# Six staging slots for the experts' weights instead of four, on one TensorE-bound core

## The chip, the core and the metric

The kernel runs on one core of one Trainium2 chip. A core has TensorE (PE; its weight loads are shown apart as PEld), VectorE (DVE), ScalarE (ACT), GpSimd (POOL) and SyncE (SP), whose queue issues most DMAs. Each engine takes its instructions in order from its own queue, and semaphores tie the queues together. The metric is the device time of one execution in microseconds; a version's time is the median of its runs.

## The reference, cut to what matters

The first step is a circular convolution along the sequence by FFT; the second is a mixture of 8 experts, of which each token uses two.

```python
X = np.fft.rfft(x, axis=1)                      # x: 8 x 2496 x 256
y = np.fft.irfft(X * F, n=x.shape[1], axis=1)   # F: the filter

logits = x @ w_gate                             # x: y as 19968 x 256
noisy_logits = logits + np.log1p(np.exp(x @ w_noise)) * noise
top2 = np.argpartition(-noisy_logits, 2, axis=1)[:, :2]
...                                             # top2_w: softmax of the two
for e in range(8):
    for k in range(2):
        mask = top2[:, k] == e
        h = np.maximum(x[mask] @ w1[e], 0.0)    # w1: 256 x 1024
        out[mask] += top2_w[mask, k, None] * (h @ w2[e])   # w2: 1024 x 256
```

## The kernel before

**Two streams.** The FFT is done batch by batch as dense transforms on PE (`s1`, `kg0` to `kg2`, `t3`, `i2`), which writes the filtered tokens to a DRAM tile `y`, computes the gates, and writes lists of token numbers per expert to a DRAM tile `lst` (`route`: a transpose on PE at L1015, a few DVE operations, and an accumulating write at L1027 on POOL's queue). As soon as lists of a batch are there, expert work on them starts (`expert`), and the FFT steps of later batches are woven into it. From some 1450 us on only expert work is left.

**Expert work.** It goes in blocks of up to 512 tokens of one expert. Per block, `read_list` loads the list (`lt`, L1048) and converts it to `ids` (L1056), `gather` fetches the tokens by an indirect DMA (L1094), `turn` transposes them (first blocks: a copy on POOL at L1146 and PE at L1154; later ones by DMA, L1125) and splits them into a high and a low part (`mxh` on ACT, L1157; `mxl` on DVE, L1158). For each eighth of the hidden layer PE makes 6 matmuls (L126 to L128) into a PSUM tile `hps`; ACT takes the ReLU `hh` (L1249) and DVE the remainder `hl` (L1250). Then PE multiplies by the second layer (`yps`; L126 to L128, and L1280 with L1281 in the later blocks), ACT scales by the gate (L1287), DVE adds in the later ones (L1289), and POOL's queue adds the rows to `out` in DRAM (L1290).

**The weights.** They come in quarters of 128 x 512 fp32 (256 KB). `front` loads four quarters of `w1` and four of `w2` for each new expert block, through `load_w`, whose DMAs stand in SP's queue (L1176; L1183 to L1191 for the smaller blocks at the end, of which `wb` at L1191 and `wc` have tiles of their own). Each quarter lands in a staging slot, ACT casts it to the high part (L1204) and DVE subtracts to get the low part (L1206). This last reading frees the slot. The cast also needs a free one of the four buffers of `w1h`/`w1l` or `w2`, which PE's matmuls on the quarter before free.

**The staging area.** `setup` makes one tile `stage`; `slot(nm)` deals out pieces of it in turn. There are four kinds: `wst` (weights, 4 slots of 512 columns), `xg` (gathered tokens, 4), `yo` (results, 4) and `x32` (transposed tokens, 2). Early on, the first 5120 columns also hold an intermediate of the FFT (`F`).

**The order.** It is partly written out by hand (`pin`, `after`), and for the rest a scheduler puts every engine's instructions in order when the kernel is built, by the waits and costs that it models. So another number of slots can move instructions on all engines. Both versions are built with `dynamic_dma_scratch_size=4096`, the ring of descriptors.

Of the kernel before, what the change touches and what calls it, by code (L numbers as in the profile page):

```python
# [10 lines left out]
F32 = mybir.dt.float32  # L11
# [43 lines left out]
YW = D + E  # L55
# [93 lines left out]
class Moe:  # L149
# [40 lines left out]
    def setup(self):  # L190
        tc, nc, io, cp = self.tc, self.nc, self.io, self.cp
        self.z = cp.tile([128, YW], F32, name="z")
        nc.gpsimd.memset(self.z, 0.0)
        self.ident = cp.tile([128, 128], F32, name="ident")
        make_identity(nc, self.ident)
        self.cV = cp.tile([128, 128], F32, name="cf")
        hl = cp.tile([128, 732], R32, name="hl")
        self.small = cp.tile([128, 64], F32, name="small")
        self.half = cp.tile([128, 4 * LR + 2 * NG + 256], F16, name="half")
        self.sum16 = cp.tile([128, 128], F16, name="sum16")  # L200
        self.new16 = cp.tile([128, 1], F16, name="new16")
        self.val16 = cp.tile([128, 2, SW], F16, name="val16")
        for t in (self.sum16, self.new16, self.val16):
            nc.gpsimd.memset(t, 0.0)
        self.fr = cp.tile([128, 2, 20, 128], F32, name="fr")
        self.fi = cp.tile([128, 2, 20, 128], F32, name="fi")
        self.wg = cp.tile([128, 2, 32], F32, name="wg")
        self.sgn = cp.tile([64, 20], F32, name="sgn")


        self.stage = cp.tile([128, 4096 + 4 * YW], F32, name="stage")
        self.turns = {}
        self.F = [self.stage[:, 2560 * h:2560 * h + 2560].rearrange("p (k b) -> p k b", k=CB) for h in range(2)]
        cm = self.P.tile([128, 494], F32, name="cm", tag="tl", bufs=3)
        self.cm = cm
        self.rC, self.rM, self.rD = cm[:RP, 0:120], cm[:, 120:248], cm[:120, 248:365]
        self.cW = cm[:, 366:494]
        self.hl = hl
        nc.vector.memset(self.wg, 0.0)
        self.cC = (hl[:RP, 0:120], hl[:RP, 120:240])  # L220
        self.cM = (hl[:, 240:368], hl[:, 368:496])
        self.cD = (hl[:120, 496:613], hl[:120, 614:731])
        sm = self.small
        self.tri, self.ones, self.key = self.half[:, -256:-128], self.half[:, -128:], sm[:, 0:8]
        self.lastok, self.iota = sm[:, 8:9], sm[:, 32:32 + SW]
        self.epart, self.ebase, self.eoff = sm[:, 9:10], sm[:, 10:11], sm[:, 16:24]
        self.base = cp.tile([128, E], F32, name="base")
        self.cnt = cp.tile([E, 1], F32, name="cnt")
        self.done = cp.tile([E, 1], F32, name="done")
        self.nblk = cp.tile([E, 1], F32, name="nblk")  # L230
        for t in (self.cnt, self.done, self.nblk):
            nc.vector.memset(t, 0.0)
        self.tab = cp.tile([1, 2, SW], F32, name="tab")

        self.rank = [cp.tile([RP, n, E], F32, name=f"rank{n}") for n in (39, 38)]
        nc.vector.memset(self.rank[0][:, :17], 0.0)
        nc.vector.memset(self.rank[1][:, :16], 0.0)

        self.pre = [cp.tile([128, 4 + E], F32, name=f"pre{i}") for i in range(2)]
        for t in self.pre:  # L240
            nc.vector.memset(t[:, :4], 0.0)

    def slot(self, nm):

        at, n, w = {"wst": (0, 4, 512), "xg": (2048, 4, YW), "yo": (2048 + 4 * YW, 4, 256), "x32": (3072 + 4 * YW, 2, 512)}[nm]
        i = self.turns[nm] = (self.turns.get(nm, -1) + 1) % n
        return self.stage[:, at + w * i:at + w * i + w]

    def load_more(self):
        nc, io = self.nc, self.io  # L250
# [334 lines left out]
    def fft_stream(self):  # L585
# [40 lines left out]
        def at(slot, g, *a):  # L626
            plan.setdefault(slot, []).append(f(g, *a))
# [781 lines left out]
```

## Time and profile before

| | us |
|---|---|
| runs | 2190.13, 2192.59, 2193.34 |
| median | 2192.59 |
| the profiled execution | 2189.98 |
| its span (first to last instruction) | 2188.3 |
| PE busy | 2149.9 (98%) |
| DVE, ACT, POOL busy | 1571.7, 1166.0, 978.4 |

The profile is of one execution. The span is what its page and its views cover; 1.7 us of the execution's time lie outside it. Idle time of an engine that is not the bottleneck costs nothing, so waits are to be read on PE first and followed from there.

### The profile page before, as it was taken

The numbers are of one execution on the slowest core, as the hardware profiler recorded it, in microseconds if no ns is written. First come the engines' busy times: TensorE is split into PE (matmuls) and PEld (weight loads), VectorE is DVE, ScalarE is ACT, GpSimd is POOL, SyncE is SP. The second block draws the span as 40 slices with busy tenths as digits, with TensorE's granted clock in tenths as the row PEclk, the third lists the DMA queues.
The fourth block names the chain that finished last, engine by engine and source line by source line (L and its number), as shares of the span: only waits on it lengthen the run. The fifth ranks groups of instructions, "written<-read, shape, count | busy, mean of one in ns | idle before, by whom it ended". The sixth has DMA issues, their size and how long they took to land.

```text
span 2188.3 us, 37937 instructions
## 1 busy us (share of the span) xinstructions
PE 2149.9 (98%) x12217; PEld 1809.9 (83%) x12217; DVE 1571.7 (72%) x3388; ACT 1166.0 (53%) x2242; POOL 978.4 (45%) x825
## 2 busy tenths in 40 slices
PE   8889999999999999999999999999999999999997
PEld 6658888888888888888888888888888888888897
DVE  4777888868877978787757976597555555665676
ACT  6565755765666456545545454444444444454565
POOL 4035345345533544454344544355444444554552
PEclk9999999999999999999999999999999999999999
DMA  9778878887987677666665667565565557687984
GB/s 250 220 216 208 222 173 206 200 196 166 224 197 182 150 162 183 146 155 156 162 129 120 160 136 165 105 128 125 121 120 115 124 109 143 151 173 159 217 205 92
DMA packets 443828, 359.55 MB, mean 164 GB/s; under 512 B 201499, under 2 KB 360963, under 8 KB 443619
## 3 DMA queue, kind: packets, MB, share of 16 engines
q1 hardware_dynamic: 382371, 272.89, 48.3%
q0 software_dynamic: 61248, 84.14, 23.4%
q8 instruction: 98, 1.61, 0.3%
q14 instruction: 111, 0.91, 0.1%
HBM read 212.85 MB, written 105.12 MB: 145 GB/s over the span
## 4 chain that ended last, share of the span: by engine, by line
PE 91%; DMA 2%; DVE 2%; ACT 2%; issue 1%; POOL 1%; SPq 0%; ACTq 0%; POOLq 0%; DVEq 0%
PE yps L1280 20%; PE hps L126 13%; PE hps L127 13%; PE hps L128 13%; PE yps L1281 10%; PE q L456 3%; PE yps L126 3%; PE yps L128 3%; PE yps L127 3%; PE q L540 2%; PE q L564 1%; PE u L492 1%; PE q L565 1%; PE q L566 1%; PE q L339 1%
## 5 line engine op out<-in xcount | busy, mean ns | idle before, releaser
L1290 POOL DMA_INDIRECT out<-stage,ids x315 | 539.2, 1712 | 376.0 <-DVE stage L1289 195.7
L1280 PE MATMUL yps<-w,hh 128*128 128x512 f32 x1944 | 682.4, 397 | 2.0 <-ACT hh L1249 1.9
L1094 POOL DMA_INDIRECT stage<-y,ids x315 | 343.8, 1091 | 510.0 <-DMA xt<-stage 401.5
L1281 PE MATMUL yps<-w,hl 128*128 128x256 f32 x1944 | 515.5, 281 | 0.0
L127 PE MATMUL hps<-mxl,w1h 128*128 128x512 f32 (+2 forms) x1312 | 506.4, 387 | 0.0
L128 PE MATMUL hps<-mxh,w1l 128*128 128x512 f32 (+2 forms) x1312 | 503.2, 385 | 0.0
L1250 DVE SCALAR_TENSOR_TENSOR hl<-hps,hh 128x512 fp32r<-128x512 f32 (+2 forms) x656 | 425.9, 663 | 105.4 <-ACT hh L1249 99.9
L126 PE MATMUL hps<-mxh,w1h 128*128 128x512 f32 (+2 forms) x1312 | 493.4, 389 | 3.5 <-DVE hl L1250 2.4
L1249 ACT ACTIVATE hh<-hps 128x512 fp32r<-128x512 f32 (+2 forms) x656 | 369.8, 583 | 209.2 <-PE hps L128 190.2
L1280 PEld LDWEIGHTS yps<-w,hh 128*128 128x128 f32 x1944 | 354.2, 188 | 74.7 <-ACT hh L1249 2.9
L1281 PEld LDWEIGHTS yps<-w,hl 128*128 128x128 f32 x1944 | 364.7, 188 | 26.3 <-DVE hl L1250 0.2
L1287 ACT ACTIVATE stage<-yps,gt 128x256 f32<-128x256 f32 x315 | 142.3, 477 | 381.1 <-PE yps L1281 192.9
L1289 DVE SCALAR_TENSOR_TENSOR stage<-yps,gt,stage 128x256 f32<-128x256 f32 x243 | 112.0, 480 | 256.7 <-ACT stage L1287 230.3
L128 PEld LDWEIGHTS hps<-mxh,w1l 128*128 128x128 f32 x1312 | 247.0, 188 | 50.8 <-issue 0.5
L127 PEld LDWEIGHTS hps<-mxl,w1h 128*128 128x128 f32 x1312 | 246.8, 188 | 42.6 <-issue 1.1
L126 PEld LDWEIGHTS hps<-mxh,w1h 128*128 128x128 f32 x1312 | 243.2, 188 | 45.8 <-DVE hl L1250 6.0
L1204 ACT CAST w1h<-stage 128x512 fp32r<-128x512 f32 x200 | 123.9, 623 | 112.8 <-DMA stage<-w 46.4
L1206 DVE TENSOR_TENSOR w1l<-stage,w1h 128x512 fp32r<-128x512 f32 x204 | 138.2, 684 | 42.4 <-ACT w1h L1204 32.4
L126 PE MATMUL yps<-w,hh 128*128 128x256 f32 x576 | 162.2, 286 | 2.1 <-ACT hh L1249 2.1
L127 PE MATMUL yps<-w,hh 128*128 128x256 f32 x576 | 159.4, 284 | 0.2 <-issue 0.2
L128 PE MATMUL yps<-w,hl 128*128 128x256 f32 x576 | 158.7, 285 | 0.1
L1206 DVE TENSOR_TENSOR w<-stage,w 128x512 fp32r<-128x512 f32 x220 | 146.4, 683 | 4.0 <-ACT w L1204 3.2
(247 smaller groups left out, 2912.2 us busy)
## 6 DMA issues: line engine op xcount, KB each, us to landing
stage<-w SPq DMA_DIRECT2D x424, 256.0 KB
x<-x SPq DMA_DIRECT2D x88, 256.0 KB
fx<-fd SPq DMA_DIRECT2D x140, 128.0 KB
fd<-c SPq DMA_DIRECT2D x73, 240.0 KB
out<-z SPq DMA_DIRECT2D x24, 702.0 KB
y<-yt SPq DMA_DIRECT2D x40, 248.6 KB
y<-yt SPq DMA_DIRECT2D x40, 234.0 KB
wb<-w SPq DMA_DIRECT2D x8, 1024.0 KB
```

The source lines that it names most:

```text
L126: nc.tensor.matmul(o, lh, rh, start=start, stop=False)
L127: nc.tensor.matmul(o, lh, rl, start=False, stop=False)
L128: return nc.tensor.matmul(o, ll, rh, start=False, stop=stop)
L1094: self.pin(lambda: nc.gpsimd.indirect_dma_start(out=x.bitcast(I32), out_offset=None, in_=self.y[:BLK + ready * ROWS], in_offset=bass.Indir ...
L1204: (cast or nc.scalar.copy)(h, sv)
L1206: nc.vector.tensor_sub(l, sv, f32v(h))
L1249: self.lastr = r = nc.scalar.activation(h, p, AF.Relu)
L1250: v = nc.vector.scalar_tensor_tensor(l, p, 0.0, f32v(h), op0=ALU.max, op1=ALU.subtract)
L1280: nc.tensor.matmul(bank, h, hl, start=(f == 0), stop=False)
L1281: self.mm = nc.tensor.matmul(p, l, hl[:, 0], start=False, stop=(f == 7))
L1287: nc.scalar.activation(o, p, AF.Copy, scale=gate[:, t])
L1290: a = nc.gpsimd.indirect_dma_start(out=self.io["out"][:BLK + ready * ROWS], out_offset=bass.IndirectOffsetOnAxis(ap=ids[:, t:t + 1], axis= ...
```

## The change

The tile `stage` gets 1024 more columns (4 KB in each partition). `wst` gets six slots instead of four: the first four stay where they were, the fifth and sixth lie behind everything else, so that no other kind of slot moves. The two new slots do not overlap the FFT's intermediate.

```diff
-        self.stage = cp.tile([128, 4096 + 4 * YW], F32, name="stage")
+        self.stage = cp.tile([128, 5120 + 4 * YW], F32, name="stage")
...
-        at, n, w = {"wst": (0, 4, 512), "xg": (2048, 4, YW), "yo": (2048 + 4 * YW, 4, 256), "x32": (3072 + 4 * YW, 2, 512)}[nm]
+        at, n, w = {"wst": (0, 6, 512), "xg": (2048, 4, YW), "yo": (2048 + 4 * YW, 4, 256), "x32": (3072 + 4 * YW, 2, 512)}[nm]
         i = self.turns[nm] = (self.turns.get(nm, -1) + 1) % n
-        return self.stage[:, at + w * i:at + w * i + w]
+        at += w * i if nm != "wst" or i < 4 else 4096 + 4 * YW + w * (i - 4)
+        return self.stage[:, at:at + w]
```

The diff adds a line, so lines behind `slot` have numbers that are one higher in the changed kernel (L1176 becomes L1177). The scheduler's order changes with it. Three places follow.

The first is SP's queue around the loads for the second expert block, between 136 and 154 us. `y<-yt` and `fd` are the FFT's writes, `stage<-w` a quarter of weights; the brackets name the semaphores that an instruction waits for. Before (the two loads are the first and second quarter of `w1`):

```order
L581 DMA y<-yt 117x4x136 [waits DMAHW6_49,Activation_49]
L581 DMA y<-yt 117x4x136 [waits DMAHW7_49,Activation_49]
L389 DMA fd<-c_1480 120x2x256 [waits DMAHW0_49,Activation_49]
L389 DMA fd<-stage 120x2x256 [waits DMAHW1_49,Activation_49]
L581 DMA y<-yt 117x4x136 [waits DMAHW2_49,Activation_49]
L1176 ISA
L1176 DMA stage<-w 128x512 [waits DMAHW3_49,DVE_49]
L581 DMA y<-yt 117x4x136 [waits DMAHW4_49,Activation_49]
L389 DMA fd<-stage 120x2x256 [waits DMAHW5_49,Activation_49]
L389 DMA fd<-c_1548 120x2x256 [waits DMAHW6_49,Activation_49]
L1176 ISA
L1176 DMA stage<-w 128x512 [waits DMAHW7_49,DVE_49]
```

Now (the three loads are the second, third and fourth quarter; the first stands four rows higher):

```order
L1177 ISA
L1177 DMA stage<-w 128x512 [waits DMAHW0_49,DVE_49]
L582 DMA y<-yt 117x4x136 [waits DMAHW1_49,Activation_49]
L390 DMA fd<-c_1480 120x2x256 [waits DMAHW2_49,Activation_49]
L390 DMA fd<-stage 120x2x256 [waits DMAHW3_49,Activation_49]
L582 DMA y<-yt 117x4x136 [waits DMAHW4_49,Activation_49]
L1177 ISA
L1177 DMA stage<-w 128x512 [waits DMAHW5_49,DVE_49]
L582 DMA y<-yt 117x4x136 [waits DMAHW6_49,Activation_49]
L390 DMA fd<-stage 120x2x256 [waits DMAHW7_49,Activation_49]
L1177 ISA
L1177 DMA stage<-w 128x512 [waits DMAHW0_49,DVE_49]
```

Two loads moved ahead of the FFT's writes, and the third and fourth quarter took the places that the first and second had.

The second is ACT's queue in the same block and the next one, from about 170 us on. `w_2435` to `w_2583` are quarters of the next `w2`, `xh` and `th` belong to the FFT. Before:

```order
L1287 ACTIVATE stage<-yps,gt 128x256 x2
L343 CAST xh<-x 117x512
L407 CAST th<-fx 128x512 x2
L343 CAST xh<-x 117x512
L388 COPY c_1822<-q_1818 120x512
L1287 ACTIVATE stage<-yps,gt 128x256
L1249 ACTIVATE hh<-hps 128x512 x2
L1204 CAST w_2435<-stage 128x512
L1204 CAST w_2488<-stage 128x512
L1204 CAST w_2530<-stage 128x512
```

Now:

```order
L1158 CAST mxh_2186<-xps 128x512
L344 CAST xh<-x 117x512
L1288 ACTIVATE stage<-yps,gt 128x256
L408 CAST th<-fx 128x512 x2
L344 CAST xh<-x 117x512
L389 COPY c_1822<-q_1818 120x512
L1205 CAST w_2435<-stage 128x512
L1205 CAST w_2488<-stage 128x512
L1205 CAST w_2530<-stage 128x512
L1288 ACTIVATE stage<-yps,gt 128x256
L1205 CAST w_2583<-stage 128x512
L1250 ACTIVATE hh<-hps 128x512 x2
```

The scaling (L1287, now L1288) moved ahead of `th`, and the casts of the `w2` quarters moved ahead of two `hh`.

The third is POOL's queue between the write of the second batch's list (`lst`) and the first tokens gathered by it, 171 to 198 us. Before:

```order
L1290 DMA out<-stage,ids 3086x256 x3
L1027 DMA lst<-ro,row 1536x128
L1048 ISA
L1048 DMA lt<-lst 128x4
...
L1290 DMA out<-stage,ids 3086x256
L1056 CAST ids<-lt 128x4 x2
L1094 DMA stage<-y,ids 128x264 x4
L1146 COPY stage<-stage 128x1024 x2
```

Now:

```order
L1291 DMA out<-stage,ids 3086x256 x3
L1028 DMA lst<-ro,row 1536x128
L1291 DMA out<-stage,ids 3086x256
L1049 ISA
L1049 DMA lt<-lst 128x4
...
L1057 CAST ids<-lt 128x4
L1095 DMA stage<-y,ids 128x264 x4
L1057 CAST ids<-lt 128x4
L1147 COPY stage<-stage 128x1024 x2
```

One write to `out` moved ahead of the reading of the list, and one of the two conversions behind the gathers.

## Rows read from the trace of the kernel before

**Rows 1.** The page, busy us of each engine with share and instructions.

```profile
PE 2149.9 (98%) x12217; PEld 1809.9 (83%) x12217; DVE 1571.7 (72%) x3388; ACT 1166.0 (53%) x2242; POOL 978.4 (45%) x825
```

**Rows 2.** Windows: length, PE, PEld, DVE, ACT, POOL busy (instructions), clock, DMA share, GB/s.

```profile
0.00:141.00 141.00, 122.22 (x713) 81.70 (x713) 89.29 (x295) 83.76 (x150) 40.29 (x52) 0.98 0.84 240
141.00:205.00 64.00, 61.39 (x384) 50.64 (x383) 52.62 (x126) 38.72 (x75) 23.35 (x21) 1.00 0.70 188
205.00:2036.00 1831.00, 1827.06 (x10282) 1552.12 (x10281) 1328.93 (x2767) 960.06 (x1832) 847.00 (x695) 1.00 0.71 157
2036.00:2188.30 152.30, 139.27 (x845) 125.47 (x843) 100.90 (x203) 83.41 (x186) 67.81 (x57) 0.98 0.73 169
```

**Rows 3.** PE's timeline (start, length), and a group of weight loads (busy, mean ns).

```profile
2003.31 0.39 PE L127 MATMUL hps<-mxl,w1h 128*128 128x512 f32 x1
2003.54 0.39 PE L128 MATMUL hps<-mxh,w1l 128*128 128x512 f32 x1
...
L128 PEld LDWEIGHTS hps<-mxh,w1l 128*128 128x128 f32 x1312 | 247.0, 188 | 50.8 <-issue 0.5
```

**Rows 4.** What SP's queue waited for: us in total, times, longest us.

```profile
SPq L1176 <- DVE w L1206: 207.1, 84, 9.6
SPq L1176 <- DVE w1l L1206: 160.1, 47, 8.5
```

**Rows 5.** The same view of ACT (first row) and of PE.

```profile
ACT w1h L1204 <- DMA stage<-w: 46.4, 44, 5.2
...
PE hps L126 <- DVE hl L1250: 2.4, 3, 1.1
PE xps L1154 <- POOL stage L1146: 2.2, 2, 1.5
PE yps L126 <- ACT hh L1249: 2.1, 1, 2.1
```

**Rows 6.** SP's timeline, the loads for the second expert block.

```profile
147.92 0.38 SPq L1176 DMA_DIRECT2D stage<-w  x1
...
153.76 0.37 SPq L1176 DMA_DIRECT2D stage<-w  x1
...
165.13 6.61 SPq L1176 DMA_DIRECT2D stage<-w  x6
```

**Rows 7.** The timeline near 169 us; brackets: idle time before, and its end.

```profile
168.65 0.62 ACT L1204 CAST w1h<-stage 128x512 fp32r<-128x512 f32 x1 [5.24 <-DMA stage<-w]
...
169.80 0.73 PE L126 MATMUL hps<-mxh,w1h 128*128 128x512 f32 x2 [0.87 <-ACT mxh L1157]
```

**Rows 8.** The timeline from the list's transpose to its first tokens' transpose, PE and POOL.

```profile
173.89 0.27 PE L1015 MATMUL ra<-ident,rx 128*56 128x128 f32 x1
...
176.62 1.86 POOL L1290 DMA_INDIRECT out<-stage,ids  x1 [1.86 <-ACT stage L1287]
178.79 2.19 POOL L1027 DMA_INDIRECT lst<-ro,row  x1 [0.31 <-DVE hl L1250]
...
188.78 0.96 POOL L1056 CAST ids<-lt 128x4 int32<-128x4 f32 x2
...
200.08 0.66 PE L1154 MATMUL xps<-ident,stage 128*128 128x128 f32 x4 [1.53 <-POOL stage L1146]
```

**Rows 9.** The timeline near 513 us, and the window behind it.

```profile
511.39 0.62 ACT L1204 CAST w<-stage 128x512 fp32r<-128x512 f32 x1 [0.86 <-PE rk L848]
...
513.44 0.58 PE L126 MATMUL yps<-w,hh 128*128 128x256 f32 x1 [2.06 <-ACT hh L1249]
...
513.40:516.70 3.30, 3.26 (x10) 2.79 (x11) 3.30 (x10) 1.47 (x3) 2.83 (x4) 0.50 0.98 223
```

**Rows 10.** The timeline near 2049 us: SP, ACT and PE.

```profile
2039.22 0.39 SPq L1191 DMA_DIRECT2D wb<-w  x1
...
2046.59 0.62 ACT L1204 CAST w1h<-wb 128x512 fp32r<-128x512 f32 x1 [5.82 <-DMA wb<-w]
...
2048.98 0.50 PE L126 MATMUL hps<-mxh,w1h 128*128 128x512 f32 x1 [1.08 <-DVE hl L1250]
```

## The prediction

> **What bounds the kernel now.** I read the busy table of the page first. TensorE is busy for 2149.9 us of a span of 2188.3 us, 98% [rows 1]; the other engines are far from full. So time can be won only where PE idles, 38.4 us in all, and the question is where that is. The windows by stage answer it [rows 2]: 18.8 us of idle time lie before 141 us (141.00 - 122.22), 2.6 us between 141 and 205 us, 3.9 us between 205 and 2036 us, and 13.0 us after that. The order of instructions, which I compared engine by engine, is the same in both kernels on PE up to about 141 us (its first 357 rows) and again from about 2035 us to the end (its last 2,123 rows, the branch that may be skipped included). What the change can reach is thus 2.6 + 3.9 = 6.5 us of idle time, and a few us that PE needs after an idle stretch.
>
> Is a busy PE also a fast one? Successive 512-column matmuls start 0.23 us apart (2003.31, 2003.54), and a weight load takes 0.188 us beside them [rows 3]; there is no gap in the stream that a load could fill. The Trainium skill speaks against this reading: "Perfetto Trace Analysis", section Identifying the Most-Contended Engine, holds that matmul busy time is a poor measure and that the busy share of weight loads shows the headroom. By it PE would have 17% of the span, some 380 us, still open (an estimate from the page's rule and the 83% of the busy table). The trace differs: 0.188 of 0.23 is 82%, so a full stream shows 83% as well.
>
> The stall that the change is aimed at is real, but it isn't PE's. SyncE's queue, which issues the weight loads at L1176, waits 207.1 us in 84 places for the split of a second-layer quarter and 160.1 us in 47 places for that of a first-layer quarter [rows 4]: the DVE subtraction that frees a staging slot. ScalarE in turn waits 46.4 us in 44 places for a landed quarter [rows 5]. PE's own list of waits holds little that comes from there: 2.4 us for `hl`, 2.2 us for gathered tokens, 2.1 us for `hh` [rows 5].
>
> **The change part by part.** Nothing is added or removed: the same loads, casts, splits and matmuls of the same sizes. It moves two things: the slot that a load waits for is now freed by the split six loads back, not four, and the scheduler puts all engines' work in another order between 141 and 2035 us. I take the places where PE waits there, and what the new order does to each.
>
> *First: 169.8 us.* PE waits 0.87 us for `mxh`, which stands on ScalarE behind the cast of the third `w1h` quarter of the second expert; that cast waited 5.24 us for its load [rows 7]. SyncE had issued the first two quarters at 147.92 and 153.76 us, when two splits had freed their slots, and the third and fourth from 165.13 us on [rows 6]. In the new order the third and fourth stand where the first two stood and wait for the same two splits, and the first two stand ahead of them and need no split of the second layer. So the third leaves some 17 us earlier, at about 148 us, and the cast finds its data. I take -0.9 us, with the ends -0.9 and 0.
>
> *Second: 200 us.* PE waits 1.53 us for the first gathered tokens whose rows come from a new list. The chain is: transpose of the list at 173.89, its write on GpSimd's queue at 178.79, its read back converted at 188.78, tokens gathered and copied, transposed at 200.08 [rows 8]; 26.2 us. On PE the order now has 49 + 63 matmuls (256 and 512 columns) and the same 8 small ones between the two transposes, where it had 70 + 59. With 0.117 us (half of the step of 0.23) and 0.23 us that is 1.5 us less cover (21 x 0.117 = 2.5 less, 4 x 0.23 = 0.9 more). The chain gets shorter as well: the write of the list waits behind an accumulating write that itself waits for ScalarE and starts at 176.62 [rows 8], and ScalarE now does the scaling for it ahead of two casts and a copy: up to 1.2 us. One conversion of ids now stands behind the gathers, half of 0.96 us. So the stall changes by between +1.5 - 1.7 = -0.2 and +1.5 us. I take +0.7.
>
> *Third: 2049 us.* PE waits 1.08 us for `hl`, because ScalarE waited 5.82 us for the load of `wb`, which SyncE issued at 2039.22 only [rows 10]. ScalarE's and PE's order are the same here. SyncE's differs a little: the staging loads and transposes ahead of `wb` wait for slots that are free two splits earlier, and the three transposes of the same block now stand behind it. If that brings 1.1 us, the stall is gone. Ends -1.1 and 0; I take half, -0.6.
>
> *Fourth: 513 us*, the dearest: 2.06 us idle because ScalarE's queue has four casts ahead of the `hh` that PE needs, and then 3.3 us at a granted clock of 0.50, the lower of the two levels, 1.2 of 2.4 GHz [rows 9]. The casts wait there for buffers of split weights that PE's own matmuls free (the row of the cast names PE), not for staging. The new order keeps them ahead of `hh`. I take 0; the lower end is -3.7 (2.06 + half of 3.3).
>
> The rest is cover. Moves of loads, casts and splits over these 1,900 us cost nothing as long as PE has work queued: ScalarE and DVE are busy 53% and 72% [rows 1], and their waits are hidden now. Should the cover be gone in a place, the price is that of the two kinds of row above: 0.9 us (169.8) to 3.7 us (513).
>
> Sum: -0.9 + 0.7 - 0.6 + 0 = -0.8 us. The profiled execution took 2189.98 us, so 2189.2 us by it. Its time is 2.6 us under the median of the runs (2192.59), so on the median I expect **2191.8 us**: no change. Within 0.2%, about what a measurement of this kernel can tell from none, is 2188.2 to 2197.0 us.
>
> **The rivals.** *Faster: the wider staging removes PE's reachable stalls.* Then 6.5 us of idle time go, 1.65 us of half clock behind 513, and the 1.1 us at 2049: 9.2 us, 2183.4 us; with half of it, 2188. For it speaks that SyncE's wait repeats 131 times. The Trainium skill would take that further: "Perfetto Trace Analysis", section Optimization Strategy, says that the same gap repeating can mean too few buffers. It asks this of the engine that should be saturated, though, and on PE no gap repeats in this stretch [rows 2, 5]. Against it: two of the larger stalls hang on the token list and on split-weight buffers. Chance 0.13.
>
> *Slower: earlier loads pull casts ahead of `hh` on ScalarE.* Its queue runs in order. In the block after 175 us it had two `hh` first and then the casts of the second layer's quarters; now four casts and a scaling stand ahead of the two `hh`. If one of these loads lands later than planned, the `hh` behind it waits, PE runs out of PSUM banks, and we have 513 once more: 3.7 us. It decides from the point where a cast waits longer than PE's queue covers: 5.24 us of waiting cost 0.87 us at 169.8 [rows 7]. One such place lies within the 0.2%; two new ones make 2191.8 + 7.4 = 2199.2 us. That ScalarE already waits 44 times for staged data, 1 us on average and almost nowhere felt on PE, speaks against it; that the new order holds for 1,900 us speaks for it. Chance 0.20.
>
> *It does not do what it says:* in the new queue most loads still wait for DVE. With six slots a load waits for an older split than with four, but a steady stream still goes at the pace of the splits. Time 2192.6 us; this lies within the forecast's bounds and shares its chance, 0.67.
>
> **How the numbers follow.** No change 0.67, faster 0.13, slower 0.20. Upward I go to 2200, past two new stalls, downward to 2185, which takes in some two thirds of the faster case: about 0.15 is left out. The ends of the known terms alone (-0.9 - 0.2 - 1.1 - 3.7 and +1.5) give 2186.7 to 2194.1, inside that. Chances of faster, same and slower by 0.2%: 0.13, 0.67, 0.20.
>
> **What would show it right or wrong.** Right: PE's busy time the same within 2 us; SyncE's wait at L1177 (L1176 of before) for DVE well below 367 us; ScalarE's wait for staged `w1h` below 46 us; no idle PE at `mxh` near 169 us; some 2 us of idle time still at the transposes near 200 us; the stall near 513 still there with its half clock. The forecast is wrong if PE shows more than 4.4 us less or more idle time between 141 and 2036 us, or if the step of 0.23 us between matmuls moves, which would mean that the wider tile changes how PE is fed.

## The result

The changed kernel takes 2206.43 us (median of 6 runs, 2202.34 to 2210.13), the kernel before 2192.69 us beside it: a ratio of **1.0062, 95% interval 1.0049 to 1.0075**. It is slower by 13.7 us, against a forecast of 2191.8 us with a range up to 2200. The profiled execution took 2206.08 us (before: 2189.98). One of the ten executions of run e15 below took 2346.26 us at a granted clock of 0.85 and is left out of its time.

The page and the windows of after, as [rows 1] and [rows 2] have them for before:

```profile
PE 2157.1 (98%) x12217; PEld 1814.3 (82%) x12217; DVE 1570.3 (71%) x3388; ACT 1167.5 (53%) x2242; POOL 970.0 (44%) x825
```

```profile
0.00:141.00 141.00, 122.92 (x712) 82.19 (x712) 88.51 (x283) 83.97 (x150) 43.14 (x54) 0.96 0.83 238
141.00:205.00 64.00, 61.09 (x380) 50.46 (x380) 53.73 (x141) 39.13 (x74) 22.30 (x22) 1.00 0.74 204
205.00:2036.00 1831.00, 1816.39 (x10196) 1541.36 (x10196) 1315.45 (x2744) 951.43 (x1815) 829.96 (x689) 1.00 0.69 156
2036.00:2204.10 168.10, 156.70 (x934) 140.29 (x932) 112.58 (x223) 92.94 (x204) 74.60 (x63) 0.99 0.71 165
```

The same 12217 matmuls keep PE busy 7.2 us longer (2157.1 against 2149.9), and it idles 47.0 us instead of 38.4. Of the idle time the stretch from 205 to 2036 us has 14.6 us (1831.00 - 1816.39) where it had 3.9; the others changed by -0.7, +0.3 and -1.6 us. So the loss sits where the order of instructions was changed and where the forecast saw nothing but cover. The waits of PE name it, and beside them those of SP and ACT that the prediction had put up as signs (us in total, times, longest):

```profile
PE yps L126 <- ACT w L1205: 5.4, 1, 5.4
...
PE yps L126 <- ACT hh L1250: 4.0, 2, 2.7
PE hps L126 <- DVE hl L1251: 3.4, 3, 1.8
```

```profile
SPq L1177 <- DVE w L1207: 307.7, 94, 10.8
SPq L1177 <- DVE w1l L1207: 159.6, 32, 8.7
...
ACT w1h L1205 <- DMA stage<-w: 21.8, 5, 10.4
```

Before, PE's list of waits had none for a cast of `w`; `hh` and `hl` stood at 2.1 and 2.4 us [rows 5]. ScalarE waits for staged `w1h` far less than before, 21.8 us in 5 places against 46.4 in 44, but one wait of the five is 10.4 us long. Three places make up most of the loss.

**Near 356 us.** The timelines of SP, ACT and PE (start, length; in brackets the idle time before and what ended it), and the windows behind the stall (columns as in [rows 2]):

```profile
348.48 3.66 SPq L1126 DMA_TRANSPOSE xt<-stage  x1
352.35 2.24 SPq L1177 DMA_DIRECT2D stage<-w  x1
```

```profile
359.39 0.62 ACT L1205 CAST w1h<-stage 128x512 fp32r<-128x512 f32 x1 [10.39 <-DMA stage<-w]
359.92 0.47 ACT L1288 ACTIVATE stage<-yps,gt 128x256 f32<-128x256 f32 x1
360.28 1.07 ACT L1250 ACTIVATE hh<-hps 128x512 fp32r<-128x512 f32 x2
361.24 0.63 ACT L1205 CAST w<-stage 128x512 fp32r<-128x512 f32 x1
```

```profile
361.92 0.58 PE L126 MATMUL yps<-w,hh 128*128 128x256 f32 x1 [5.38 <-ACT w L1205]
```

```profile
361.90:366.50 4.60, 4.58 (x18) 3.27 (x18) 4.41 (x9) 4.00 (x8) 2.64 (x3) 0.50 0.63 135
366.60:400.00 33.40, 33.40 (x211) 29.43 (x211) 27.17 (x64) 20.40 (x39) 12.53 (x11) 1.00 0.80 198
```

ScalarE stands still for 10.39 us in front of the cast of the *next* block's first `w1` quarter, whose load SyncE could issue only at 352.35, behind a transposing DMA. Behind that cast in the same queue stand a scaling, two `hh` and the cast of the *current* block's first `w2` quarter, and PE needs those: it idles 5.38 us and then runs 4.6 us at a granted clock of 0.50, the lower level. That is 5.4 + 4.6/2 = 7.7 us. In the kernel before, the same cast started at 362.19, behind all that work; it waited 2.09 us for its load, and PE idled nowhere near. ScalarE's order of instructions at this place, first before, then after (numbers mark the tiles):

```
L1287 ACTIVATE stage_89<-yps_5014,gt_4166
L1249 ACTIVATE hh_5206<-hps_5199
L1249 ACTIVATE hh_5239<-hps_5232
L1204 CAST w2_5243<-stage_89
... (hh, two casts of w2, a scaling, the last cast of w2, hh, xh)
L1204 CAST w1h_5550<-stage_89
```

```
L1204 CAST w1h_5550<-stage_89
L1287 ACTIVATE stage_89<-yps_5014,gt_4166
L1249 ACTIVATE hh_5206<-hps_5199
L1249 ACTIVATE hh_5239<-hps_5232
L1204 CAST w2_5243<-stage_89
```

**Near 517 us**, the place of [rows 9] (ACT, PE, window):

```profile
515.91 1.28 ACT L824 ACT_TABLE_LOAD   x1
517.21 0.22 ACT L824 ACTIVATE ge<-gd 117x22 f32<-117x22 f32 x1
517.34 1.64 ACT L1205 CAST w<-stage 128x512 fp32r<-128x512 f32 x3
...
519.76 0.59 ACT L1250 ACTIVATE hh<-hps 128x512 fp32r<-128x512 f32 x1
```

```profile
520.40 0.58 PE L126 MATMUL yps<-w,hh 128*128 128x256 f32 x1 [2.74 <-ACT hh L1250]
522.99 0.79 PE L126 MATMUL hps<-mxh,w1h 128*128 128x512 f32 x1 [1.23 <-DVE hl L1251]
```

```profile
520.40:525.80 5.40, 4.17 (x14) 3.41 (x15) 5.36 (x15) 1.68 (x4) 1.96 (x2) 0.50 0.91 250
```

The router's exponential with its table load now stands between the scaling and the casts. Before, it ran ahead of that scaling, while ScalarE had nothing else to do:

```profile
505.32 0.22 ACT L823 ACTIVATE ge<-gd 117x22 f32<-117x22 f32 x1 [0.69 <-DVE gd L822]
507.12 0.47 ACT L1287 ACTIVATE stage<-yps,gt 128x256 f32<-128x256 f32 x1 [1.58 <-issue]
```

The place costs 2.74 + 1.23 + 4.17/2 = 6.1 us instead of 3.7.

**Near 708 us** a reciprocal of the router, four splits and two other operations stand ahead of `hl` on DVE, which works without a break from 704.92 us on (DVE, PE, window):

```profile
704.92 1.24 DVE L799 RECIPROCAL rank<-rank 117x176 f32<-117x176 f32 x1
...
708.70 0.68 DVE L1207 TENSOR_TENSOR w<-stage,w 128x512 fp32r<-128x512 f32 x1
709.30 1.27 DVE L1251 SCALAR_TENSOR_TENSOR hl<-hps,hh 128x512 fp32r<-128x512 f32 x2
```

```profile
710.03 0.50 PE L126 MATMUL hps<-mxh,w1h 128*128 128x512 f32 x1 [1.84 <-DVE hl L1251]
```

```profile
711.70:715.00 3.30, 3.30 (x11) 2.64 (x10) 2.85 (x6) 0.60 (x1) 0.00 (x0) 0.51 0.31 115
```

That is 1.84 + 3.3/2 = 3.5 us. Five small stalls between 561 and 974 us (1.27, 0.48, 0.63, 0.45 and 0.21 us) add 3 us. The sum, 7.7 + 2.4 + 3.5 + 3 = 16.6, less the 2 us that two of the predicted terms gave back, is 14.6 of the 15.8 us between the two spans. Left out are a new wait of 1.07 us for `mxl` at 142.50 us and the 1.01 us for `hl` at 1437 us that is gone; they cancel.

### The profile page after: what moved, and what is told of

Its sections match the earlier page's. It is cut to its first block, busy times and chain, and to the rows that moved or that the text cites. A ratio compares the mean times of both kernels' runs of the same rounds, so it can differ in the third digit from the quotient of the medians.

```text
span 2204.1 us, 37935 instructions
## 1 busy us (share of the span) xinstructions
PE 2157.1 (98%) x12217; PEld 1814.3 (82%) x12217; DVE 1570.3 (71%) x3388; ACT 1167.5 (53%) x2242; POOL 970.0 (44%) x825
## 4 chain that ended last, share of the span: by engine, by line
PE 90%; DVE 4%; issue 2%; ACT 2%; DMA 2%; POOL 0%; SPq 0%; another core or an unknown queue 0%; POOLq 0%; ACTq 0%; DVEq 0%
PE yps L1281 20%; PE hps L126 13%; PE hps L127 13%; PE hps L128 12%; PE yps L1282 10%; PE q L457 3%; PE yps L126 3%; PE yps L128 3%; PE yps L127 3%; PE q L541 2%; PE u L493 1%; PE q L565 1%; PE q L566 1%; PE q L567 1%; PE q L420 1%
## 5 line engine op out<-in xcount | busy, mean ns | idle before, releaser
L1291 POOL DMA_INDIRECT out<-stage,ids x315 | 523.8, 1663 | 488.6 <-DVE stage L1290 286.3
L128 PE MATMUL hps<-mxh,w1l 128*128 128x512 f32 (+2 forms) x1312 | 504.1, 385 | 0.0
L126 PE MATMUL hps<-mxh,w1h 128*128 128x512 f32 (+2 forms) x1312 | 493.8, 390 | 3.5 <-DVE hl L1251 3.4
L1288 ACT ACTIVATE stage<-yps,gt 128x256 f32<-128x256 f32 x315 | 142.7, 478 | 375.4 <-PE yps L1282 182.5
L128 PEld LDWEIGHTS hps<-mxh,w1l 128*128 128x128 f32 x1312 | 247.5, 189 | 51.0 <-issue 0.6
L126 PEld LDWEIGHTS hps<-mxh,w1h 128*128 128x128 f32 x1312 | 243.8, 189 | 44.7 <-DVE hl L1251 6.1
L126 PE MATMUL yps<-w,hh 128*128 128x256 f32 x576 | 163.5, 287 | 9.6 <-ACT w L1205 5.4
L128 PE MATMUL yps<-w,hl 128*128 128x256 f32 x576 | 159.0, 285 | 0.0
```

Of the source, the lines that this page charges most:

```text
L126: nc.tensor.matmul(o, lh, rh, start=start, stop=False)
L128: return nc.tensor.matmul(o, ll, rh, start=False, stop=stop)
L1288: nc.scalar.activation(o, p, AF.Copy, scale=gate[:, t])
L1291: a = nc.gpsimd.indirect_dma_start(out=self.io["out"][:BLK + ready * ROWS], out_offset=bass.IndirectOffsetOnAxis(ap=ids[:, t:t + 1], axis= ...
```

## The experiments

The runs stand on several chips, on which the kernel before differs by up to 8 us, so each time stands beside the kernel before on the same chip. What was expected of e1 to e4 is in us of a chip on which the kernel before takes 2192.6. Where a list binds the order, the line numbers of the kernel's body are 9 to 11 higher, and those of the matmuls (L126 to L128) 2 higher.

| run | weight slots, order | us | before | ratio, 95% interval |
|---|---|---|---|---|
| e1 | 4, wider tile, old order | 2183.60 | 2184.60 | 0.9992 (0.9983 to 1.0002) |
| e2 | 6, old order on all engines | 2182.56 | 2184.60 | 0.9991 (0.9982 to 1.0000) |
| e3 | 6, old order, SyncE free | 2180.73 | 2184.60 | 0.9983 (0.9973 to 0.9992) |
| e4 | 5, free | 2200.28 | 2184.60 | 1.0065 (1.0050 to 1.0081) |
| e5 | 6, the change's order | 2206.94 | 2191.89 | 1.0072 (1.0045 to 1.0099) |
| e6 | e5, one cast back | 2198.69 | 2191.89 | 1.0029 (1.0019 to 1.0040) |
| e7 | e5, one load forward | 2199.85 | 2191.89 | 1.0039 (1.0026 to 1.0051) |
| e8 | e5, three places | 2197.96 | 2191.89 | 1.0031 (1.0021 to 1.0042) |
| e9 | 4, pace 61 | 2192.06 | 2191.47 | 1.0004 (0.9993 to 1.0016) |
| e10 | 4, pace 198 | 2191.55 | 2191.47 | 0.9999 (0.9988 to 1.0011) |
| e11 | 4, pace 116 | 2192.04 | 2191.47 | 1.0004 (0.9988 to 1.0019) |
| e12 | 6, pace 61 | 2207.37 | 2191.47 | 1.0079 (1.0055 to 1.0104) |
| e13 | e3, one cast put forward | 2188.49 | 2184.74 | 1.0018 (1.0006 to 1.0030) |
| e14 | 6, rule on casts | 2182.34 | 2184.74 | 0.9993 (0.9984 to 1.0003) |
| e15 | 4, rule on casts | 2187.74 | 2184.74 | 1.0023 (1.0012 to 1.0034) |
| e16 | 6, looser rule | 2189.64 | 2184.74 | 1.0020 (1.0005 to 1.0035) |
| e17 | e14 again | 2191.01 | 2192.39 | 0.9989 (0.9979 to 0.9999) |
| e18 | 6, harder rule | 2239.10 | 2192.39 | 1.0226 (1.0211 to 1.0240) |

### Slots, room or order

e1 is the change with `"wst": (0, 4, 512)`, e4 with `"wst": (0, 5, 512)`. In e2 and e3 a list of instruction numbers per engine, taken from the kernel before, binds the scheduler:

```diff
+        for t in LISTED.values():
+            seq = [by[f"I-{n}"] for n in t]
+            for a, b in zip(seq, seq[1:]):
+                self.tc.add_manual_dep(b, a.name, ..., reason="order as listed")
```

> The wider staging tile alone: 5120 columns beside the gathered rows as in the change, but still four weight slots at their old places. Every engine's instructions stand in the same order as in the kernel before. Theory (the order of the in-order queues made the change slow, the room costs nothing): 2190 to 2195 us, the same as before. Rival (the wider tile or the moved addresses of what lies behind it cost time by themselves): 2203 to 2209 us, like the change.

> Six weight slots as in the change, but each engine's instructions, SyncE's too, are bound to the order that they had in the kernel before; only the waits for a free slot are shorter. Theory (order alone): no stall near 356 us, none near 708 us, the stall near 513 us as before; 2189 to 2193 us. Rival (more loads in flight collide with other transfers, and this makes the change slow): 2200 to 2208 us although the order is the old one.

> Six weight slots, with PE, ScalarE, VectorE and GpSimd bound to the order of the kernel before; SyncE alone is left to the scheduler, which moves 367 of its instructions. Theory (a cast that stands ahead of hh on ScalarE): with no such cast 2189 to 2194 us, however SyncE is ordered. Rival (SyncE's order of loads and transposes is what costs): stalls on loads in front of the casts, 2198 to 2208 us.

> Five weight slots, the scheduler free as in the change. It moves 141 of ScalarE's instructions against 232 with six. Theory (order, and so the luck of the places where a cast or a router's step lands ahead of hh): each such place 3 to 7 us, none to two of them, 2188 to 2205 us, and every place is found as a stall of PE behind a cast, split or router's step; nothing between them. Rival (a price for each slot, by more loads in flight): half of the change's loss, 2199 us, spread over the run and not in two or three stalls.

The room costs nothing (e1), and six slots in the old order lose nothing (e2, e3), so neither the addresses nor more loads in flight are the cause. Free ordering of SyncE does no harm either, though its queue waits almost as long in e3 as in the change (453 us against 467):

```profile
SPq L1186 <- DVE w L1216: 280.8, 109, 11.3
SPq L1186 <- DVE w1l L1216: 172.1, 52, 7.9
```

The stretch from 205 to 2036 us of e2, e3 and e4:

```profile
205.00:2036.00 1831.00, 1829.65 (x10303) 1555.00 (x10302) 1329.11 (x2770) 960.11 (x1835) 847.27 (x696) 1.00 0.70 158
```

```profile
205.00:2036.00 1831.00, 1830.40 (x10314) 1556.38 (x10313) 1331.10 (x2772) 962.45 (x1836) 845.91 (x699) 1.00 0.70 158
```

```profile
205.00:2036.00 1831.00, 1821.66 (x10235) 1547.86 (x10234) 1316.96 (x2751) 954.18 (x1820) 827.54 (x691) 1.00 0.70 156
```

PE idles 1.4 and 0.6 us there with six slots in the old order, 9.3 us with five in their own. Five lose as much as six; the price is not one per slot. At 15.7 us over the kernel before, e4 lies above both of its ranges, which ended some 12 and 6 us over it. What is left is the order. The stall near 513 us, which e2 was expected to keep, does not show in its profiled execution.

### Which places

In e5 to e8 the list is the change's own order, with rows moved: none (e5); the cast `w1h_5550` and its split behind the four casts and splits of the current `w2` (e6); its load ahead of the four transposing DMAs (e7); e6 and the two router places mended by hand (e8).

> The change itself, every engine bound by a list to the very order that it has in the change: the control for the next three, on their chip. Both theories: the change's loss again, 11 to 16 us over the kernel before, with PE idle some 5 us near 356 us, some 4 us near 517 to 522 us and some 2 us near 708 us.

> The order of the change with one instruction of ScalarE moved: the cast of the next expert's first quarter of w1, which stands ahead of one output's scaling, two hh and four casts of w2, goes behind them (its split on VectorE goes behind theirs). Theory (this one cast, waiting for its load, held up hh and w2): the stall near 356 us and the half-clock steps behind it go, 7 us less than the control. Rival (that cast is only the first to show a load that comes late, and the next to need it stalls PE instead): at most 2 us less.

> The order of the change with one instruction of SyncE moved: the load for that same cast goes ahead of the four transposing DMAs and the four other transfers that stood in front of it. The cast stays ahead of hh and w2. Theory (a cast ahead of hh costs only where its load is late): the load is there in time, the stall near 356 us goes as in the last one, 6 to 7 us less than the control. Rival (the place of the cast costs by itself, late load or not): still 3 us or more of PE idle there.

> The order of the change mended by hand at all three places: the cast as above; near 517 us hh ahead of the router's exponential with its table load on ScalarE, and hl and two splits ahead of the chain that waits for it on VectorE; near 708 us hh between the casts of w2 on ScalarE, and hl ahead of a reciprocal and the remaining splits on VectorE. 37 of the engines' instructions at most stand elsewhere than in the change. Theory (these three places are the change's whole loss): 15 to 20 us under the control, 3 us under to 3 us over the kernel before. Rival (the loss is spread over many places, the three are samples): 5 us or more over the kernel before.

One cast of ScalarE moved, with its split on VectorE, is worth 8.3 us (2206.94 - 2198.69), one load of SyncE 7.1 us; the sum above gave 7.7. e5 has only four executions, from 2201.18 to 2211.34 us, so both differences are known to some 5 us only. Near 356 us PE waits for nothing in e6, and 0.45 us at 360.06 in e7. In e7 the load goes out at 344.25 and the cast, though still ahead of `hh` and `w2`, starts after 0.85 us that no load ended (SP, then ACT):

```profile
344.25 0.33 SPq L1187 DMA_DIRECT2D stage<-w  x1
```

```profile
352.81 0.62 ACT L1215 CAST w1h<-stage 128x512 fp32r<-128x512 f32 x1 [0.85 <-issue]
```

So this cast ahead of `hh` does next to no harm as long as its load is there, and costs 7 to 8 us when the load is late. e8 missed its mark: 0.7 us under e6, where 7 to 12 us were expected, and 6.1 us over the kernel before, as the rival had it. My mending turned the old waits near 513 us into new ones, for the scaling that I had put behind `hh` and for the router's sum that I had put behind `hl` (PE):

```profile
514.65 0.38 PE L128 MATMUL yps<-w,hh 128*128 128x256 f32 x1 [1.34 <-ACT stage L1298]
516.92 0.17 PE L857 MATMUL rk<-sum,half 128*128 128x8 f16 x1 [1.76 <-DVE sum L841]
557.58 0.39 PE L128 MATMUL yps<-w,hh 128*128 128x256 f32 x1 [2.43 <-ACT hh L1260]
```

What these two places cost for good is thus not measured one by one.

### Any new order, or that of more slots

My theory was now that any order that nobody picked for its time would lose as much. One number of the table that paces the transform among the blocks (`PACE = {0: 110, 1: 200, 2: 60}`, `PACES = 115`) moves, with four slots, 137 (e9), 243 (e10) or 212 (e11) of ScalarE's instructions, where the change moves 230.

> Four weight slots, and one number of the table that paces the transform's steps among the experts' blocks moved by one (61 for 60 while the third batch's blocks run). No work is added or left out; the scheduler makes another order from it, with 137 of ScalarE's and 240 of VectorE's instructions elsewhere than before (the change moves 230 and 427). Theory (the loss is that of any order that was not picked for its time, the slots only made a new one): 3 to 20 us over the kernel before, in stalls like those of the change. Rival (the freedom that more slots give, casts of w1 ahead of w2 and hh, is what costs): within 4 us of the kernel before.

> As the last one, with another number of the same table: 198 for 200 while the second batch's blocks run, four slots; 243 of ScalarE's and 394 of VectorE's instructions stand elsewhere. Theory (any unpicked order): 3 to 20 us over the kernel before. Rival (freedom of the slots): within 4 us of it.

> As the last two, with the pace of the later batches 116 for 115, four slots; 212 of ScalarE's and 462 of VectorE's instructions stand elsewhere, all after the first three batches. Theory (any unpicked order): 1 to 15 us over the kernel before, the earlier stalls of the change absent. Rival (freedom of the slots): within 4 us of it.

> Six weight slots with the number 61 for 60: the change's own order nudged in the same way. Theory (any unpicked order): anywhere from 0 to 25 us over the kernel before, with the stall near 356 us there or not as the new order has it, so no steady price of six slots over four. Rival (freedom of the slots): 10 to 17 us over the kernel before, as the change is, since the freedom is the same.

The theory fell: three new orders with four slots lie within 0.05% of the kernel before, and the nudged order with six slots loses 0.8% with the stall of the change at its old place (PE), and with waits of 2.75, 1.24 and 1.83 us at the two other places:

```profile
359.44 0.58 PE L126 MATMUL yps<-w,hh 128*128 128x256 f32 x1 [4.94 <-ACT w L1204]
```

Near 520 us the four-slot orders wait for `hh` too: 2.15 us in e9, 1.67 in e10, 3.25 in e11. So that wait is not one of more slots; what the change adds there is mainly the 1.23 us for `hl`. The profiled executions of e10 and e11, 4.3 and 6.7 us over their medians, idle 9.2 and 9.9 us between 205 and 2036 us, in waits of at most 3.3 us. So the idle time of one execution doesn't rank kernels; the medians do.

What the orders with four slots share, and those with more do not, can be counted in ScalarE's order. With four slots `w1` and `w2` take turns in the same four places, so the load of quarter q of the next `w1` waits until quarter q of the current `w2` is split, and its cast cannot stand ahead of that one. In the kernel before and in e9, e10 and e11, 7 casts of `w1` stand ahead of some cast of an older `w2` (ahead of 25 in all); in the change, in e4 and in e12 it is 30 (ahead of 114). These counts are of the whole program, with the branch that may be skipped; of the casts that the traces hold it is 2 (ahead of 5) and 25 (ahead of 94).

### The lost dependency

e13 is e3 with `w1h_5550`, and its split on VectorE, put where the change has it. e14 and e15 forbid such casts, e16 only between equal quarters, e18 ahead of the last `hh` too:

```diff
+        c = (cast or nc.scalar.copy)(h, sv)
+        if nm == "w2":
+            self.w2c = c
...
-            with self.after(... else None):
+            with self.after(... else self.w2c):
```

(e16 keeps one `w2c` for each quarter; e18 has the last `hh` of the current block in its place.)

> Six weight slots, PE, ScalarE, VectorE and GpSimd in the order of the kernel before and SyncE left to the scheduler, as in the second run with that order, but with the one cast of the next expert's w1 put where the change has it: ahead of one output's scaling, two hh and four casts of w2 (its split ahead of the first hl). Theory (a cast whose load is late, ahead of hh): a stall of PE of 5 to 6 us near 356 us and half-clock steps behind it, 6 to 9 us over the run without it, 2 to 6 us over the kernel before. Rival (it only hurts together with the change's other moves): no stall there, 4 to 0 us under the kernel before.

> Six weight slots, the scheduler free but for one rule: on ScalarE no cast of the next expert's w1 before the last cast of the current expert's w2. It stands so ahead of 7 w2-holding casts in the kernel before, of 30 in the change, of none here. Theory (the dependency that four slots had, and that kept w1's casts behind w2's, is what was lost): within 4 us of the kernel before. Rival (the shifted places of the router's steps, not the casts, are most of it): 6 to 16 us over it.

> The same rule with four weight slots: the control for the last one. Theory: within 4 us of the kernel before and of the last run. Rival (the rule itself delays casts and stalls PE): 5 us or more over the kernel before.

> Six weight slots and a looser rule: the cast of quarter q of the next expert's w1 not before the cast of quarter q of the current w2, which four slots had as a dependency (with four slots the rule moves five instructions of ScalarE). 29 casts of w1 still stand ahead of some cast of w2, but of 84 in all against 114. Theory (the lost dependency): within 5 us of the kernel before. Rival (the shifted router's steps): 6 to 16 us over it.

One cast put forward into the old order brings the stall back: 0.35% over e3 by the two ratios, which are of two chips, or 7.7 us of 2184.7 (ACT, PE, window):

```profile
358.57 0.62 ACT L1214 CAST w1h<-stage 128x512 fp32r<-128x512 f32 x1 [9.81 <-DMA stage<-w]
```

```profile
361.10 0.58 PE L128 MATMUL yps<-w,hh 128*128 128x256 f32 x1 [4.81 <-ACT w L1214]
```

```profile
361.10:366.00 4.90, 4.90 (x20) 3.38 (x21) 4.48 (x8) 3.46 (x7) 2.43 (x4) 0.50 0.65 138
```

With the rule, six slots are back at the kernel before or a little under it: 0.9993 where the change has 1.0062, the stalls at the router's places gone as well. PE's only listed wait in the long stretch of e14:

```profile
PE yps L126 <- ACT stage L1289: 1.0, 1, 1.0
```

That is e14's fastest execution. The one profiled of e17, the same kernel, idles 6.1 us in this stretch, with no wait over 1.7 us and none of the change's stalls.

The same rule with four slots lies 0.30% above e14, by intervals that do not meet, or 5.4 us by the medians; it was expected within 4 us. So under this rule the six-slot kernel is the faster one. Why is not shown: the two differ in their orders as well as in their slots, and the only profiled execution of e15 is its fastest, with 3.6 us of idle time in the long stretch. The looser rule e16 leaves `w1`'s first quarter ahead of `w2`'s second, and one such cast waits for its load again (ACT, then PE):

```profile
366.99 0.62 ACT L1204 CAST w1h<-stage 128x512 fp32r<-128x512 f32 x1 [11.30 <-DMA stage<-w]
```

```profile
369.56 0.58 PE L126 MATMUL yps<-w,hh 128*128 128x256 f32 x1 [8.65 <-ACT stage L1289]
```

It is 4.9 us over the kernel before, just inside what the theory allowed. That this stall is the cause is likely but not measured: the profiled execution is the slowest of eight, 8.4 us over the median. So the order that the four-slot dependency fixed between equal quarters, put back alone, does not bring the old order back: 24 casts of `w1` that the trace holds still stand ahead of some older cast of `w2`, against 2 in the kernel before.

> The kernel of the six-slot run with the rule once more, with more rounds, since it looked like the best of all: by the theory 0 to 6 us under the kernel before (the two stalls on late loads that the prediction counted, 1.5 us, and the one near 513 us, up to 5 us, gone); by the rival (the earlier run was chance) at it or above it.

> Six weight slots and the harder rule: no cast of the next expert's w1 ahead of the current expert's last hh. Casts of w1 stand ahead of 183 hh in all, against 944 in the change and 852 with the rule before. Theory (only a cast whose load is late does harm, and with w2's casts first the loads are there): no further gain, and where all four casts come in a row behind the last hh PE may wait for the first split: 0 to 8 us over the run with the softer rule. Rival (each cast ahead of hh costs something): 2 us or more under it.

e17 puts the rule 0.1% under the kernel before, at the edge of what can be told from no change. e18 says nothing on `hh`: its new order also put 18 zero-filling stores ahead of the transform's first transfers on SyncE, and of the 47 us that it lost PE idles 36.7 at one place (SP, PE):

```profile
32.94 45.25 SPq L307 DMA_DIRECT2D out<-z  x18
```

```profile
88.20 3.74 PE L339 MATMUL q<-x,cm 117*120 117x512 f32 x4 [36.72 <-DMA x<-x]
```

Whether casts ahead of `hh` alone cost anything stays open.

## Why the prediction was wrong

**What bounds the kernel** was right: PE, with an unchanged step between matmuls (0.23 us, 367.06 to 367.29 in the changed kernel), and the time lost is its idle time and what the clock takes behind it.

**The terms** were right in direction. *First*: no idle time at `mxh` near 169 us is left (predicted -0.9; it was 0.87), though the new waits at 142.50 (1.07 us) and 186.78 us (0.49) outweigh it, and the stretch to 205 us gains nothing. *Second*: 1.34 us before the transposes at 198.60, 0.2 us less than the 1.53 of [rows 8], at the end of its bounds. *Third*: the stall for `hl` at 2049 us is gone, -1.1 where I took half.

```profile
198.60 0.66 PE L1155 MATMUL xps<-ident,stage 128*128 128x128 f32 x4 [1.34 <-POOL stage L1147]
```

Together some -2 us. e2 and e3, with six slots in the old order, show the first and the third gone and the second as it was, 1.53 us. They are 0.1 to 0.2% under the kernel before, where e1 without any more slots is 0.1% under it, so the gain can hardly be told from nothing.

*Fourth* (near 513 us) I took at 0; the casts stay ahead of `hh` as said, but the router's exponential joined them, and the place went from 3.7 to 6.1 us. It is a place on the edge: e1, e2 and e3, with the old order, don't show it at all in their profiled executions.

**"The rest is cover" is the step that failed.** It put the moved casts and splits at nothing as long as PE has work queued, since ScalarE and VectorE are busy 53% and 72% and their waits are hidden now; against the rival it held that ScalarE's 44 waits for staged data were hardly felt on PE. But a wait that is hidden in one order says nothing of another. In the kernel before, the cast at 362.19 waited 2.09 us behind the work that PE needed next; in the change the same cast stands ahead of that work, waits 10.39 us, and the place costs 7.7 us. With the place near 708 us and the small ones (3.5 and 3 us) the term at nothing measures some 14 us. I priced the four-slot ring as a wait and did not see that it was an order as well. With it gone, 30 casts instead of 7 stand ahead of older `w2` casts; five wait for their load, and one of the five is late enough to stall PE.

Shown for this place is that the cast ahead of the current work, with a late load, makes the stall (e6, e7, e13), and for the loss as a whole that it lies in the order (e2, e3) and goes when no cast of `w1` may pass one of `w2` (e14, e17). That the lost dependency alone makes the order bad is not shown: e16 puts back the order that it fixed, between equal quarters, and is 4.9 us slow.

**The rival "earlier loads pull casts ahead of `hh`"** named the mechanism, the engine and the price's kind, and e6, e7 and e13 show it, down to the condition that the load must be late. It looked for it in the wrong place: at casts of `w2` in the block after 175 us, where PE waits for no `hh`, and not at the next expert's `w1`. Its price was too small, 3.7 us a place, from the one row at 513, where this one is 7.7. And it is about half of the loss: at 517 and 708 us no late load shows, but steps of the router ahead of `hh` and `hl`. Its chance, 0.20, rested on the same misread 44 waits.

**The signs.** ScalarE's wait for staged `w1h` fell below 46 us as foretold, while the kernel became slower; SyncE's wait at L1177 did not fall below 367 us but rose to 467 (307.7 + 159.6), and is 453 in e3, one of the fastest kernels here. Presumably a queue that gets to its loads sooner waits longer at them; no run tests this. Neither sum was a sign of the time. PE's busy time (+7.2 us, against 2 allowed) and its idle time between 141 and 2036 us (17.5 against 6.5, 4.4 more allowed) were, and both said wrong. Of the rival "faster" little is left: no run is more than 0.2% under the kernel before, and the gap that repeated was SyncE's.

The Trainium skill (page "Perfetto Trace Analysis", section Optimization Strategy) says that a gap that repeats on the engine that should be saturated can mean too few buffers. PE, that engine here, had no such gap, so no run here tests it.

What stays open: why the router's steps moved as far as they did near 517 and 708 us. The rule of e14 takes these stalls away too, but no run moved them alone without making a new wait.

## What to carry over

A ring of buffers does two things: it makes loads wait, and through the load it fixes where the work that empties a buffer can stand in an in-order queue. Before widening one under a scheduler, look in the new order for work on the *next* item that now stands ahead of work on the *current* one, and ask of each whether its load can be late; if the freedom isn't wanted, keep the order with a rule and take only the buffers. Judge by the waits of the engine that bounds, one by one: totals of waits on queues that run ahead can rise while the kernel gets faster.

## What the runs showed of the hardware

A long idle stretch of PE cost more than itself. In the change and in e13, 5.38, 4.81 and 1.84 us of idle time were each followed by 3.3 to 4.9 us at a granted clock of 0.50 or 0.51, the lower of the two levels, while 1.27 us near 562 us and 1.34 us near 198 us left the window around them at 1.00:

```profile
561.50:565.00 3.50, 2.22 (x21) 1.66 (x19) 2.98 (x7) 3.50 (x8) 0.00 (x0) 1.00 1.22 193
```

The length of the stretch alone does not settle it: 1.81 us near 219 us in e1 left the clock at 1.00, and 1.68 us near 563 us in e5 was followed by a window at 0.69.

The weight load at 352.35 us held SyncE's queue for 2.24 us where others take 0.37 us [rows 6]; that, and the 3.66 us of the transpose before it, is part of why the load was late. What made it so slow is open. It stands right behind a transposing DMA, but so do 55 other weight loads of the same trace, and none of those took more than 0.65 us; other loads of over 2 us stand behind plain transfers.
